# Linear attention and a mish FFN on one core: a staging room for the last group of part 1, and the first seven forms of part 2 spread over seven slots

## The chip, the cores and the metric

The kernel runs on one core of a Trainium2 chip. The metric is the device time of an execution in microseconds (us), the median of several runs. Engines are named as in the profile: PE (TensorE), DVE (VectorE), ACT (ScalarE), POOL (GpSimd), SP (SyncE). DMA transfers are issued here from SP and from ACT; each of the two has its own queue.

## What is computed

Two stages, on 8 batches, 8 heads, 576 positions and 64 columns a head, which make 4608 tokens of 512 columns:

```python
kv = np.einsum('bhsd,bhse->bhde', k, v)
out = np.einsum('bhsd,bhde->bhse', q, kv)
rms = np.sqrt(np.mean(out * out, axis=-1, keepdims=True) + 1e-06)
x = out / rms * g_norm                     # then (4608, 512)
h = x @ w_in                               # (4608, 2048)
g = h * np.tanh(np.log1p(np.exp(h)))       # mish
return g @ w_out                           # (4608, 512)
```

## The kernel before

Both products of the FFN are taken apart by a scheme with seven products of half-size blocks in place of eight. Each side of a product comes in seven "forms": `A11`, `S1`, `S2`, `A12`, `S4`, `S3`, `A22` (the order of `MADE`) for the activations, others for the weights. Four of them are blocks of the matrix, three are sums or differences of blocks. Each form is split into a high part (a cast on ACT, L117) and the rest (a subtraction on DVE, L118), and each product is three products of such parts on PE.

**Part 1** makes `g = mish(x @ w_in)` and writes it to DRAM (`gd`). It goes over nine tiles of 512 tokens, and in each over four column groups: 36 groups, "the last group" being the 36th. A group takes seven slots (`group`, p0 to p6), in each of which PE runs 12 products. In p2 a group also finishes the previous group's seventh product; the last group's seventh product follows at the very end by itself (`last_product`). Two tables, `plan` and `evict`, say which work of the other engines is written into which slot: `slot` first writes the evictions that are due, then the products, then the planned work. Every engine executes its instructions in the order in which they are written, so a slot is a place in each engine's order and not a time.

The result of a group is gathered in three staging tiles of the pool `up`: `ula` (block 11), `ulb` (block 21) and `ur` (blocks 12 and 22). Each name has two buffers, so a group reuses the buffers of the group two before it. ACT copies the first partial products into them (L460, L465, L474), DVE adds the others (L518), ACT takes the mish (L114, for `ulb` straight out of the PSUM bank), and three stores to `gd` follow (`put_in`: L521 for `ula`, L516 for `ulb`, L524 for `ur`, called the right store). In the last tile ACT issues these stores, elsewhere SP.

**Part 2** makes `g @ w_out` in 18 groups of 256 tokens. Its weights are in DRAM as forms already (`wod`) and come in eight loads (`wo_load`, L687), each into a buffer of `wfp` that part 1 has ceased to read. The first group of part 2 (`gs[0]`) goes over the contraction in four pairs of chunks (L815), pair 0 to pair 3, so that PE can begin before all weights are there. The forms of pair 0 are made in slot 18 of part 1's last tile, all seven at once (`g_pair`), in a room of their own (`g0`). Pairs 1 to 3 take two rooms each from `gf_room`: first the one for the forms `A11` to `A12`, then the one for the other three. `gf_room` deals out the four rooms of the pool `fp`, which part 1 has used for `x` and its forms, and one room of a pool `fp2`, in a cycle of five; the room of `fp2` comes first, sixth and so on. From the second group on (L733) each form takes one room, and ACT and DVE make forms three products ahead of PE (`AHEAD`). After each form `A22` SP loads the activations of a group further on (`g_load`, L692).

Each DMA counts on one of eight semaphores (DMAHW0 to DMAHW7 below). A transfer's issue also waits until an earlier transfer on the same semaphore has landed, where the engine doesn't know that already.

Of the kernel before, what the change touches and what calls it, by code (L numbers as in the profile page):

```python
# [7 lines left out]
F32 = mybir.dt.float32  # L8
F32R = mybir.dt.float32r
# [13 lines left out]
MADE = (A11, S1, S2, A12, S4, S3, A22)  # L23
# [3 lines left out]
def linear_attention_rms_mish_ffn(  # L27
# [38 lines left out]
    P = 128  # L66
    R = 32
    T = 512
    TH = T // 2
    NT = NTOK // T  # L70
# [3 lines left out]
    NQ = NF2 // 2  # L74
# [12 lines left out]
    fp = ctx.enter_context(tc.tile_pool(name="fp", bufs=4))  # L87
    fq = ctx.enter_context(tc.tile_pool(name="fq", bufs=1))
    up = ctx.enter_context(tc.tile_pool(name="up", bufs=2))
# [7 lines left out]
    pools = {}  # L97
# [18 lines left out]
    def split(hi, lo, src):  # L116
        nc.scalar.copy(hi, src)  # L117
        nc.vector.tensor_sub(lo, src, hi.bitcast(F32))  # L118
# [322 lines left out]
    def at(t, f):  # L441
        plan.setdefault(t, []).append(f)
# [59 lines left out]
    def u_dst(st, block):  # L502


        name, shape = {"11": ("la", TH), "21": ("lb", TH)}.get(block, ("r", T))
        if name not in st:
            st[name] = up.tile([P, 2, shape], F32, name="u" + name)
        return st[name] if name != "r" else st[name][:, :, (int(block[0]) - 1) * TH:int(block[0]) * TH]

    def put_in(st, block, bank, t):  # L510
        o, i, n = u_dst(st, block), st["i"], st["n"]
        eng = nc.sync if i < NT - 1 else nc.scalar
        left, right = gd[i][:, 2 * n:2 * n + 2, :], gd[i][:, NF2 + 2 * n:NF2 + 2 * n + 2, :]
        if block == "21":
            mish(o, bank)
            at(t + 2, lambda: eng.dma_start(left[:, :, TH:T], o))  # L516
            return
        nc.vector.tensor_add(o, bank, o)  # L518
        if block == "11":
            then(t + 1, lambda: mish(o, o))  # L520
            at(t + 3, lambda: eng.dma_start(left[:, :, 0:TH], o))  # L521
        elif block == "22":
            then(t + 1, lambda: mish(st["r"], st["r"]))
            at(t + 3, lambda: eng.dma_start(right, st["r"]))  # L524
# [147 lines left out]
    gs = [{"s": s, "f": {}, "bank": lambda name: ps_m.tile([P, 2, TH], F32, name=name)[:, 0]} for s in range(NG)]  # L672
    rooms_made = 0
# [6 lines left out]
    def gf_room():  # L680
        nonlocal rooms_made
        rooms_made += 1
        return (fp if rooms_made % 5 != 1 else pools["fp2"]).tile([P, 4, 2, 2, P], F32R, name="gf")

    def wo_load(c):
        wo[c] = wfp.tile([P, 7, 2, G], F32R, name="wf")
# [2 lines left out]
    def g_load(s):  # L689
        g = gs[s]["g"] = pools["gp"].tile([P, NFC, G], F32, name="g")  # L690
        i, h = divmod(s, T // G)
        nc.sync.dma_start(g, gd[i][:, :, h * G:(h + 1) * G])  # L692

    def g_block(st, f, cs):
        if f == S1:
            if st["s"] == 0:
                if cs.start not in st:
                    st[cs.start] = pools["g0"].tile([P, 2, P], F32, name="g1")
                return st[cs.start]
            if f not in st:  # L700
                st[f] = fq.tile([P, NF2, P], F32, name="a22")
            return st[f][:, cs]
        r, h = {A11: (0, 0), S2: (0, 0), A12: (1, 0), S4: (1, 0), S3: (0, 1), A22: (1, 1)}[f]
        return st["g"][:, r * NF2 + cs.start:r * NF2 + cs.stop, h * P:(h + 1) * P]

    def g_form(st, f, cs, t):

        a11, a12, a21, a22 = (g_block(st, f_, cs) for f_ in (A11, A12, S3, A22))
        if f == S1:
            nc.vector.tensor_add(g_block(st, S1, cs), a21, a22)  # L710
            nc.vector.tensor_sub(a21, a11, a21)
        elif f == S2:
            nc.vector.tensor_sub(a11, g_block(st, S1, cs), a11)  # L713
        elif f == S4:
            nc.vector.tensor_sub(a12, a12, a11)
        split(t[:, 0], t[:, 1], g_block(st, f, cs))
        return t

    def g_make(st, f):

        st["f"][f] = g_form(st, f, slice(0, NF2), gf_room().rearrange("p f s c n -> p (f s c n)").rearrange("p (s c n) -> p s c n", s=2, c=NF2))

    def g_pair(st, n, rooms):

        cs = slice(2 * n, 2 * n + 2)
        for f in MADE:
            st["f"][f, n] = g_form(st, f, cs, rooms[f // 4][:, f % 4])
# [38 lines left out]
    def pair_rooms(n):  # L766
        if n == 0:
            return [pools["g0"].tile([P, m, 2, 2, P], F32R, name=f"g{m}") for m in (4, 3)]
        return [gf_room() for _ in range(2)]


    t8 = NS * (NT - 1)
    at(t8 + 6, part2)
    at(t8 + 7, lambda: g_load(0))
    at(t8 + 8, lambda: g_load(1))
    at(t8 + 18, lambda: g_pair(gs[0], 0, pair_rooms(0)))
    for n in range(NQ - 1):
        for m in range(2):
            at(t8 + 7 * n + 10, lambda c=2 * n + m: wo_load(c))
# [2 lines left out]
    for i in range(NT):  # L782
        for n in range(NQ):
            st = {"i": i, "n": n, "bank": bank_new}
            t = NS * i + 7 * n
            for p, f in enumerate(group(st, t, mm_in, u_dst, put_in, prev)):
                slot(t + p, f)
            prev = st
# [14 lines left out]
    st = gs[0]  # L803
    for n in range(NF2 // 2):
        if n + 1 < NF2 // 2:
            g_pair(st, n + 1, pair_rooms(n + 1))
        for c in range(2):
# [3 lines left out]
            for (left, right), (b, h) in where.items():  # L811
                gf = st["f"][left, n]
# [92 lines left out]
```

## Time and profile before

| | us |
|---|---|
| median of 3 runs | 890.3 (888.53 to 890.5) |
| the profiled execution | 890.41 |
| its span, first to last instruction | 888.6 |
| part 2's first product (L815) | 517.86 |
| part 2's second group begins (L733) | 538.16 |

The mean granted clock of PE is 0.992. Times of the trace are counted from the first instruction, so 1.8 us of the profiled execution's time lie outside of them. In a row of the timeline stand start, duration, engine, line, operation, target and sources, and in brackets the idle time of the engine ahead of it with what ended it. "ACTq" and "SPq" are DMA issues. A row can hold several instructions of one kind (x12).

### The profile page before, as it was taken

Reading aid. Unit: us, or ns where it says so; the run is one execution under the profiler, and the core shown is the slowest. Engines: PE = TensorE matmul, PEld = TensorE weight load, DVE = VectorE, ACT = ScalarE, POOL = GpSimd, SP = SyncE. Lnnn points to the kernel's source line nnn. Section 1 sums busy time; section 2 is a strip of 40 time slices with the busy share of each in tenths; the row PEclk is TensorE's granted clock in tenths of the full one; section 3 lists DMA queues with packets and bytes.
Section 4 is the critical chain, followed back from the end, with each engine's and each line's share of the span. In section 5 each row is a group of like instructions: output and inputs, shape, how many; then the busy total and the mean of one; then the engine's idle time right before and its main releaser. Section 6 shows DMA issues by size and latency. Waiting matters only on the chain.

```text
span 888.6 us, 17122 instructions
## 1 busy us (share of the span) xinstructions
PE 827.8 (93%) x7004; PEld 793.5 (89%) x7004; DVE 614.2 (69%) x808; ACT 460.3 (52%) x698; POOL 4.3 (0%) x21
## 2 busy tenths in 40 slices
PE   1767899988999999999999899999999999999997
PEld 1456699988999999999899799999999999999997
DVE  4798685776777677777764358876766667776772
ACT  2565657566566765676665344434444443434431
POOL 1000000000000000000000000000000000000000
PEclk9999999999999999999999999999999999999999
DMA  9848598887979797767567994344444443334421
GB/s 285 252 134 259 154 291 253 254 254 232 284 231 301 226 270 213 215 205 213 192 202 241 420 421 151 119 128 154 152 137 124 134 124 119 119 119 135 153 69 48
DMA packets 154766, 177.42 MB, mean 200 GB/s; under 512 B 17408, under 2 KB 135168, under 8 KB 153664
## 3 DMA queue, kind: packets, MB, share of 16 engines
q1 hardware_dynamic: 151088, 170.59, 62.1%
q10 hardware_dynamic: 3600, 5.74, 1.9%
q8 instruction: 55, 0.90, 0.4%
q14 instruction: 23, 0.19, 0.1%
HBM read 114.30 MB, written 62.00 MB: 198 GB/s over the span
## 4 chain that ended last, share of the span: by engine, by line
PE 62%; DMA 13%; DVE 10%; ACT 8%; issue 4%; SPq 2%; ACTq 0%; DVEq 0%
PE a L733 21%; PE bc L733 16%; PE a L497 13%; PE bc L497 7%; DMA gd<-ula 4%; PE s L248 2%; DMA vm<-in_v_dram 2%; DVE ur L518 1%; DMA wf<-in_q_dram 1%; DMA gd<-ur 1%; DVE gf L118 1%; DMA wf<-in_k_dram 1%; ACT L382 1%; ACT gf L117 1%; DMA rd<-fl 1%
## 5 line engine op out<-in xcount | busy, mean ns | idle before, releaser
L733 PE MATMUL a<-wf,gf 128*128 128x256 f32 x1632 | 201.8, 283 | 0.5 <-DVE ur L764 0.5
L733 PEld LDWEIGHTS a<-wf,gf 128*128 128x128 f32 x1632 | 198.4, 192 | 0.7 <-DVE ur L764 0.7
L118 DVE TENSOR_TENSOR gf<-g,gf 128x1024 fp32r<-128x1024 f32 (+1 forms) x123 | 132.9, 1087 | 89.4 <-ACT gf L117 89.4
L497 PE MATMUL a<-gf,wf 128*128 128x256 f32 x1296 | 173.6, 288 | 9.8 <-ACT ur L474 4.4
L497 PEld LDWEIGHTS a<-gf,wf 128*128 128x128 f32 x1296 | 163.5, 193 | 16.9 <-ACT ur L474 6.9
L497 PE MATMUL bc<-gf,wf 128*128 128x256 f32 x1296 | 171.7, 285 | 7.0 <-DVE ula L518 2.6
L497 PEld LDWEIGHTS bc<-gf,wf 128*128 128x128 f32 x1296 | 162.4, 192 | 9.0 <-DVE ula L518 2.9
L117 ACT CAST gf<-g 128x1024 fp32r<-128x1024 f32 (+1 forms) x123 | 114.5, 939 | 93.4 <-DVE g L713 65.1
L733 PE MATMUL bc<-wf,gf 128*128 128x256 f32 x1224 | 152.7, 283 | 1.3 <-DVE gf L118 1.3
L733 PEld LDWEIGHTS bc<-wf,gf 128*128 128x128 f32 x1224 | 149.3, 192 | 1.7 <-ACT gf L117 1.0
L497 PE MATMUL a<-a,wf 128*128 128x256 f32 x432 | 58.5, 285 | 4.7 <-DVE ur L518 4.7
L497 PEld LDWEIGHTS a<-a,wf 128*128 128x128 f32 x432 | 54.7, 191 | 8.9 <-DVE ur L518 5.4
L114 ACT ACTIVATE ur<-ur 128x1024 f32<-128x1024 f32 x36 | 38.1, 1058 | 37.5 <-DVE ur L518 37.5
L118 DVE TENSOR_TENSOR fa<-fl,fh 128x1024 fp32r<-128x1024 f32 x28 | 34.2, 1223 | 20.7 <-ACT fh L117 19.7
L118 DVE TENSOR_TENSOR gf<-gf 128x512 fp32r<-128x512 f32 x45 | 30.4, 690 | 22.7 <-ACT gf L117 22.7
L117 ACT CAST gf<-a 128x1024 fp32r<-128x1024 f32 x17 | 17.9, 1052 | 53.4 <-DVE a L710 50.9
L465 ACT COPY ur<-bc 128x512 f32<-128x512 f32 (+1 forms) x53 | 27.4, 517 | 31.2 <-PE bc L733 23.0
L117 ACT CAST gf<-gf 128x512 fp32r<-128x512 f32 x45 | 27.1, 618 | 31.8 <-DVE gf L421 19.1
L474 ACT COPY ur<-a 128x512 f32<-128x512 f32 (+1 forms) x53 | 27.3, 515 | 30.3 <-PE a L733 24.6
L518 DVE TENSOR_TENSOR ula<-bc,ula 128x512 f32<-128x512 f32 x36 | 24.8, 688 | 24.7 <-PE bc L497 24.5
L114 ACT ACTIVATE ula<-ula 128x512 f32<-128x512 f32 x36 | 22.8, 633 | 22.1 <-DVE ula L518 22.1
L518 DVE TENSOR_TENSOR ur<-bc,ur 128x512 f32<-128x512 f32 x36 | 24.4, 678 | 11.1 <-PE bc L497 5.9
(128 smaller groups left out, 849.5 us busy)
## 6 DMA issues: line engine op xcount, KB each, us to landing
g<-gd SPq DMA_DIRECT2D x18, 2048.0 KB, 8.7
gd<-ur SPq DMA_DIRECT2D x32, 512.0 KB, 3.5
wod<-wst SPq DMA_DIRECT2D x16, 896.0 KB, 6.1
wf<-wod SPq DMA_DIRECT2D x8, 1792.0 KB, 15.4
gd<-ula SPq DMA_DIRECT2D x32, 256.0 KB, 5.5
gd<-ulb SPq DMA_DIRECT2D x32, 256.0 KB, 4.8
w<-in_moe_w_out_dram SPq DMA_DIRECT2D x32, 256.0 KB, 4.9
km<-in_k_dram SPq DMA_DIRECT2D x28, 256.0 KB, 4.3
```

The costliest lines, as they stand in the source:

```text
L114: nc.scalar.activation(o, i, AF.Mish)
L117: nc.scalar.copy(hi, src)
L118: nc.vector.tensor_sub(lo, src, hi.bitcast(F32))
L248: nc.tensor.matmul(kvps[o * D:(o + 1) * D, b % 2, h0 // 2 + i, :], kt, vt, start=(c == 0), stop=(c == CM))
L382: nc.scalar.preload_act_table_set("natural_log_exp_and_others")
L465: then(t + 2, lambda: nc.scalar.copy(dst(st, "22"), st["c"]))
L474: then(t + 4, lambda: nc.scalar.copy(dst(st, "12"), st["a"]))
L497: nc.tensor.matmul(bank[:, jj], w[:, right, a, kc, :], xf[:, b, kc, :], start=first and jj == kc == s == 0, stop=(kc == 1 and s == 2), ski ...
L518: nc.vector.tensor_add(o, bank, o)
L733: nc.tensor.matmul(bank, gf[:, a, c, :], wo[c][:, right, b, :], start=first and c == s == 0, stop=(c == NF2 - 1 and s == 2), skip_group_ch ...
```

## The change

Three edits. The last group's `la` and `r` no longer take buffers of `up`: one room of `fp2` of 1536 columns holds both. Its `lb` stays in `up`. `gf_room` takes the room of `fp2` as the fifth of the cycle and no longer as the first. And the seven forms of pair 0 are written one to a slot, in slots 17 to 23 of the last tile, in place of all in slot 18.

```diff
         if name not in st:
-            st[name] = up.tile([P, 2, shape], F32, name="u" + name)
+            if (st["i"], st["n"]) == (NT - 1, NQ - 1) and name != "lb":
+                if "room" not in st:
+                    st["room"] = pools["fp2"].tile([P, 2, 3 * TH], F32, name="gf")
+                st[name] = st["room"][:, :, 0:TH] if name == "la" else st["room"][:, :, TH:]
+            else:
+                st[name] = up.tile([P, 2, shape], F32, name="u" + name)
...
-        return (fp if rooms_made % 5 != 1 else pools["fp2"]).tile([P, 4, 2, 2, P], F32R, name="gf")
+        return (fp if rooms_made % 5 else pools["fp2"]).tile([P, 4, 2, 2, P], F32R, name="gf")
...
-    at(t8 + 18, lambda: g_pair(gs[0], 0, pair_rooms(0)))
+    first_rooms = []
+    for n, f in enumerate(MADE):
+        def first_form(f=f):
+            if f == MADE[0]:
+                first_rooms.extend(pair_rooms(0))
+            gs[0]["f"][f, 0] = g_form(gs[0], f, slice(0, 2), first_rooms[f // 4][:, f % 4])
+        at(t8 + 17 + n, first_form)
```

The order on PE and on SP stays as it was, row by row; only line numbers differ (from L518 on by 5, part 2's by 5 to 11). On DVE and ACT three places change.

DVE at the end of part 1, before: the second-to-last group's three additions (`ula`, `ur`, `ur`) behind the seven forms of pair 0. The tiles `g_` are the rooms of pair 0.

```order
L118 TENSOR_TENSOR g_5685<-g,g_5685 128x256 [waits DMAHW6_49,Activation_49]
L710 TENSOR_TENSOR g_5689<-g 128x256 [waits DMAHW7_49]
L711 TENSOR_TENSOR g<-g 128x2x128 [waits DVE_49]
L118 TENSOR_TENSOR g_5685<-g_5689,g_5685 128x256 [waits Activation_49]
L713 TENSOR_TENSOR g<-g_5689,g 128x2x128 [waits DVE_49]
L118 TENSOR_TENSOR g_5685<-g,g_5685 128x256 [waits Activation_49]
L118 TENSOR_TENSOR g_5686<-g,g_5686 128x256 [waits Activation_49]
L715 TENSOR_TENSOR g<-g 128x2x128 [waits DVE_49]
L118 TENSOR_TENSOR g_5685<-g,g_5685 128x256 [waits Activation_49]
L118 TENSOR_TENSOR g_5686<-g,g_5686 128x256 [waits Activation_49] x2
L518 TENSOR_TENSOR ula<-bc,ula 128x512 [waits DMAHW0_49,PE_49]
L518 TENSOR_TENSOR ur<-bc,ur 128x2x256 [waits DMAHW3_49,PE_49]
```

The same place on DVE now:

```order
L118 TENSOR_TENSOR g_5666<-g,g_5666 128x256 [waits DMAHW6_49,Activation_49]
L715 TENSOR_TENSOR g_5689<-g 128x256 [waits DMAHW7_49]
L716 TENSOR_TENSOR g<-g 128x2x128 [waits DVE_49]
L118 TENSOR_TENSOR g_5666<-g_5689,g_5666 128x256 [waits Activation_49]
L523 TENSOR_TENSOR ula<-bc,ula 128x512 [waits DMAHW0_49,PE_49]
L718 TENSOR_TENSOR g<-g_5689,g 128x2x128 [waits DVE_49]
L118 TENSOR_TENSOR g_5666<-g,g_5666 128x256 [waits Activation_49]
L523 TENSOR_TENSOR ur<-bc,ur 128x2x256 [waits DMAHW3_49,PE_49]
L118 TENSOR_TENSOR g_5667<-g,g_5667 128x256 [waits Activation_49]
L523 TENSOR_TENSOR ur<-a,ur 128x2x256 [waits PE_49]
```

The addition to `ula` stands behind the forms `A11` and `S1` alone, and the other two additions each behind one form more.

ACT in the last group of part 1, before: its copies out of the banks, and the issues of the second-to-last group's stores.

```order
L460 COPY ula<-a 128x512 [waits DMAHW5_49,PE_49]
L521 DMA gd_102<-ula 128x2x256 [waits DMAHW2_49,Activation_49]
L465 COPY ur<-bc 128x2x256 [waits DMAHW0_49,PE_49]
L114 ACTIVATE ulb<-a 128x512 [waits DMAHW4_49,PE_49]
L524 DMA gd_102<-ur 128x1024 [waits Activation_49]
L474 COPY ur<-a 128x2x256 [waits PE_49]
L516 DMA gd_102<-ulb 128x2x256 [waits DMAHW6_49,Activation_49]
```

The same now, from the copy into the new room (`gf`) on:

```order
L460 COPY gf<-a 128x2x256 [waits PE_49]
L117 CAST g_5667<-g 128x256
L526 DMA gd_102<-ula 128x2x256 [waits DMAHW2_49,Activation_49]
L465 COPY gf<-bc 128x2x256 [waits PE_49]
L117 CAST g_5667<-g 128x256
L114 ACTIVATE ulb<-a 128x512 [waits DMAHW4_49,PE_49]
L529 DMA gd_102<-ur 128x1024 [waits DMAHW5_49,Activation_49]
L474 COPY gf<-a 128x2x256 [waits PE_49]
L521 DMA gd_102<-ulb 128x2x256 [waits DMAHW6_49,Activation_49]
```

The two copies have lost their waits for a store, and the issue of the `ur` store has got the wait on DMAHW5 that the first copy had before; two casts of pair 0's forms now stand among them.

ACT at the beginning of part 2, before: the end of pair 2's casts, the last group's right store and its `ulb` store, and pair 3's first casts.

```order
L117 CAST gf<-g 128x256 x2
L524 DMA gd_102<-ur 128x1024 [waits DMAHW2_49,Activation_49]
L516 DMA gd_102<-ulb 128x2x256 [waits DMAHW3_49,Activation_49]
L117 CAST gf<-g 128x256
L117 CAST gf<-g_5997 128x256 [waits DVE_49]
```

The same now:

```order
L117 CAST gf<-g 128x256 x2
L529 DMA gd_102<-gf 128x2x512 [waits DMAHW2_49,Activation_49]
L521 DMA gd_102<-ulb 128x2x256 [waits DMAHW3_49,Activation_49]
L117 CAST gf<-g 128x256 [waits DMAHW2_49,DMAHW1_49]
L117 CAST gf<-g_5996 128x256 [waits DVE_49]
```

Pair 3's first cast has got two waits: DMAHW2 is the semaphore of the right store two rows above it, DMAHW1 that of the last group's `la` store.

## The prediction

> **What bounds the kernel now.** I read the page first, then TensorE's (PE's) timeline where part 1 passes into part 2, then ScalarE's (ACT's) there, then the chain of waits, then the landing times of the transfers. The page:
>
> ```profile
> span 888.6 us, 17122 instructions
> PE 827.8 (93%) x7004; PEld 793.5 (89%) x7004; DVE 614.2 (69%) x808; ACT 460.3 (52%) x698; POOL 4.3 (0%) x21
> gd<-ur SPq DMA_DIRECT2D x32, 512.0 KB, 3.5
> ```
>
> PE is busy for 93% of the span, so the change can only act where PE stands idle. PE's timeline around the passage (start, duration, what ended the idle time before):
>
> ```profile
> 497.38 3.04 PE L497 MATMUL a<-gf,wf 128*128 128x256 f32 x24
> 501.53 1.70 PE L497 MATMUL bc<-gf,wf 128*128 128x256 f32 x12 [1.12 <-DVE ula L518]
> 505.40 1.70 PE L497 MATMUL a<-gf,wf 128*128 128x256 f32 x12 [0.74 <-ACT ula L460]
> 510.91 2.33 PE L497 MATMUL bc<-gf,wf 128*128 128x256 f32 x12 [2.37 <-ACT ur L465]
> 513.04 2.50 PE L497 MATMUL a<-gf,wf 128*128 128x256 f32 x12
> 516.32 1.70 PE L497 MATMUL a<-a,wf 128*128 128x256 f32 x12 [0.78 <-DVE ur L518]
> 517.86 5.20 PE L815 MATMUL q<-wf,g 128*128 128x256 f32 x42
> 522.90 15.42 PE L815 MATMUL q<-wf,gf 128*128 128x256 f32 x126
> 538.16 3.04 PE L733 MATMUL a<-wf,gf 128*128 128x256 f32 x24
> 543.92 3.04 PE L733 MATMUL a<-wf,gf 128*128 128x256 f32 x24
> 547.44 3.10 PE L733 MATMUL bc<-wf,gf 128*128 128x256 f32 x24 [0.48 <-DVE gf L118]
> 551.37 3.10 PE L733 MATMUL bc<-wf,gf 128*128 128x256 f32 x24 [0.84 <-DVE gf L118]
> ```
>
> Four idle pieces stand in the last group of part 1 (1.12 + 0.74 + 2.37 + 0.78 = 5.01 us), none in the 20.3 us of L815, and two small ones in part 2's second group, where VectorE (DVE) makes the forms too late. What matters is which chain ends last at 551.37. The chain of waits there:
>
> ```profile
> 490.44 14.25 DMA gd<-ula
> 504.77 0.04 ACT ula L460
> 504.85 22.89 DMA gd<-ula
> 527.81 0.34 ACTq L524
> 528.24 0.42 ACTq L516
> 528.70 0.41 ACT gf L117
> 534.86 1.22 DVE gf L118
> ...
> 551.37 3.10 PE bc L733 x24
> ```
>
> The idle time in part 1 is not on it. It runs through two stores of the last tile: ACT can't issue the last group's right store (L524) until the store issued at 504.85 has landed at 527.74, and the forms of pair 3 (from 528.70) and of the second group stand behind that on ACT and DVE. So the passage is held by slow stores, and a gain in part 1 reaches the end only if this chain gets shorter as well.
>
> **The change part by part.**
>
> *One form per slot.* Before, seven forms stand in one block on DVE, and the evictions of the group before the last stand behind them; PE then waits 1.12 us at 501.53. With one form per slot (a slot is 12 products, half of the 3.04 us at 497.38), the addition to `ula` stands behind two forms, not seven, and is done before PE asks for that bank. No instruction is added. The 1.12 us go. Three slots of ACT take a little longer in their place, since the mish of that group and the copy that PE waits for at 505.40 now stand among casts of 0.4 us and behind the `ulb` store's issue; I leave the 0.74 us where they are (bounds 0 and 0.9).
>
> *Own staging.* It takes away the waits of ACT on the stores of two groups earlier (rows of ACT, then two stretches with each engine's busy time and, ahead of the last two columns, the granted clock):
>
> ```profile
> 499.41 0.37 ACTq L516 DMA_DIRECT2D gd<-ulb  x1
> 504.77 0.58 ACT L460 COPY ula<-a 128x512 f32<-128x512 f32 x1 [1.00 <-DMA gd<-ula]
> 510.28 0.58 ACT L465 COPY ur<-bc 128x512 f32<-128x512 f32 x1 [4.92 <-DMA gd<-ur]
> 521.78 0.58 ACT L114 ACTIVATE ulb<-a 128x512 f32<-128x512 f32 x1
> 528.70 0.41 ACT L117 CAST gf<-g 128x256 fp32r<-128x256 f32 x1 [1.28 <-DMA gd<-ula]
> 506.00:511.00 5.00, 2.63 (x23) 2.42 (x21) 0.69 (x1) 0.72 (x2) 0.00 (x0) 1.00 1.03 435
> 511.00:515.00 4.00, 4.00 (x22) 4.00 (x23) 0.69 (x1) 1.73 (x4) 0.00 (x0) 0.58 1.00 422
> ```
>
> The copy at 510.28 need no longer wait, so PE's 2.37 us go. With them goes a slow stretch: behind that idle time the granted clock is 0.58 (511 to 515), and 24 products take 513.04 + 2.50 - 510.91 = 4.63 us where the 24 at 497.38 take 3.04: 1.59 us. The 0.78 us at 516.32 stay, because the last product follows directly on the one whose bank DVE must read first. Part 2 then begins 1.12 + 2.37 + 1.59 = 5.1 us earlier, at about 512.8 in place of 517.86 (5.8 us earlier if the 0.74 go too).
>
> The Trainium skill ("TensorE: Matmul & The Clock Gate", "Part 1: The HAM clock gate") says that the clock falls to half after an idle window of some 3.4 us and comes back after such a window of work. Here the trace differs in the first half: 2.37 us of idle time in one piece were enough. By the rule alone there would be no slow stretch to win back, and part 2 would begin 3.5 us earlier in place of 5.1; the end, below, hangs on neither.
>
> *What of the 5.1 us survives.* Three things catch it, in this order. First, `ulb` is not restaged: the last mish (521.78 before) goes into the buffer that an earlier `ulb` store, issued at 499.4, still empties. ACT's stores land in their order here: the one ahead at 510.2 and the one behind at 527.74. I estimate its landing in the middle, at 519. Pair 2's forms, which stand behind this mish, so begin 521.78 - 519 = 2.8 us earlier, not 5.1. Second, the weights of part 2 still come over a full DMA:
>
> ```profile
> wf<-wod SPq DMA_DIRECT2D x1, 1792.0 KB, 15.3
> 518.06 0.32 SPq L687 DMA_DIRECT2D wf<-wod  x1
> gd<-ur ACTq DMA_DIRECT2D x1, 512.0 KB, 8.0
> gd<-ur ACTq DMA_DIRECT2D x1, 512.0 KB, 16.9
> 533.30 1.09 DVE L118 TENSOR_TENSOR gf<-g,gf 128x256 fp32r<-128x256 f32 x3 [0.47 <-ACT gf L117]
> 534.42 0.52 SPq L692 DMA_DIRECT2D g<-gd  x1
> 490.00:500.00 10.00, 10.00 (x85) 10.00 (x85) 3.35 (x9) 5.04 (x12) 0.00 (x0) 1.00 1.06 422
> 525.00:530.00 5.00, 5.00 (x44) 5.00 (x44) 3.11 (x9) 1.92 (x7) 0.00 (x0) 1.00 0.99 417
> 534.00:537.00 3.00, 3.00 (x26) 2.91 (x26) 2.53 (x4) 0.82 (x1) 0.00 (x0) 1.00 0.61 191
> ```
>
> The landing times are each the only one of its kind in a narrow window: the weight load of 518.06, the right store of 527.81, and the right store issued at 493.3. The last two columns of the window rows are the DMA engines' share and GB/s: full from 490 to 530 at 417 to 422 GB/s, free after about 534. The last weight load, issued at 518.06, lands 15.3 us later, at 533.4. Issued earlier, it still stands behind the same bytes, so its landing stays. PE needs it for the last eighth of L815's 168 products (20.3 us, so 2.5 us), and L815 can't end before 533.4 + 2.5 = 535.9: 2.3 us ahead of 538.16. That is a ceiling on any gain at this place.
>
> *The new wait.* The room is now the fifth in the cycle of rooms, the first of pair 3's two, and holds the last group's `la` and `r` until their stores have landed. So the first cast of pair 3 on ACT waits for the landing of the right store, the very store that could only be issued at 527.81. Before, that cast waited for the issue alone. Behind it on ACT stand the six other casts of pair 3, those of the second group and the copy out of L815's banks; DVE's subtractions wait for the casts one by one, PE for DVE, and SP's next load of the activations (534.42) for DVE's last read of the old ones. The profile has this store's time: issued at 527.81, landed 8.0 us later (third row), at 535.8. Its issue doesn't move, since it hangs on the store of 504.85: that one is issued at about 504.2 instead, but in ACT's queue it stays behind the two stores ahead, of which the nearer lands at about 519 either way, beside the same weight loads. So the cast starts at 527.8 + 8.0 + 0.1 = 535.9, where it started at 528.70: 7.2 us later. The bounds: 3.5 us to landing, the median of such a store on SP's queue (the page's row), gives 531.4 and 2.7 us; 16.9 us, the longest of the kind here (from 493.3 to 510.2, with weight loads all the way), gives 544.8 and 16.1 us. I take 8.0, because it is the same store against the same queue, which empties at about 534. In the changed layout its rows are 2 KB and no longer 4 KB; at a rate set by bytes that costs nothing, and I allow 0.5 us.
>
> *From there to the end.* Pair 3 takes the same instructions, 528.70 to 534.39 (the row at 533.30), now 535.9 to 541.6. PE has finished pair 2 at about 528 and stands idle for some 8 us, then goes at the pace of the forms; its last half of pair 3 (2.5 us) ends at about 544.4. The second group's forms follow on DVE as before, 7.2 us later; the load at 534.42 and its reader, the third group's first form, move alike. Their partner in the chain, the product at 551.37, comes at 558.6. PE at 544.4 has the 5.8 us of the first two products ahead of it and then meets the third form, before at 543.92 and now at 551.1 at the latest: it waits for DVE, not DVE for it. After 551.37 PE had 0.5 us of idle time in all, so nothing there gives the 7.2 us back.
>
> The sum against the profiled execution (890.41 us, of which 888.6 are the span): 890.41 + 7.2 = 897.6 us. The median of the three runs is 890.3, 0.1 us from it, so I let the number stand.
>
> **The rivals.**
>
> *The store lands in time (faster).* If the right store had landed by 528.7, the new wait would cost nothing, and the ceiling of the weights would decide: 890.4 - 2.3 = 888.1 us. For it speak the 5.1 us that part 1 surely saves. Against it: the store's issue at 527.81 and the shortest landing on the page, 3.5 us. It decides only if the store of 504.85 lands before about 520, some 8 us sooner than it did. Chance 0.05. Part of the way (the cast at 528 to 530) gives no change, 0.05.
>
> *The queue is empty sooner.* If the right store meets no weight load, it takes 3.5 us, and the cast comes 2.7 us later: 893.1 us. Against it: the last weight load lands at 533.4, so the store has company till then. The Trainium skill ("DMA: Bandwidth & Descriptors", "Queues, rings and completion order") says that a DMA engine takes turns between the rings that have work, a whole packet of some 9 to 17 descriptors at a turn; by that rule 256 KB in rows of 1 KB, 16 to an engine, would be through in about two turns. The trace speaks against so quick a passage: 22.89 us for the store at 504.85. Chance 0.09.
>
> *PE becomes the bound after its idle time (slower still).* After 8 us of idle time a slow stretch like that of 511 to 515 is to be expected. At half speed PE's last 2.5 us of pair 3 become 5, and another 3 us of work may take 6: L815 ends at 547 to 549 and the third product of the second group starts at 553 to 555 in place of 551.1. Part of that is hidden by the later forms, since DVE is late there; I put 1 to 3 us on top: 899 to 900.5. Chance 0.11. It decides when L815 ends later than about 546.
>
> **How the numbers follow.** My forecast, the new wait at its measured length, has a chance of 0.70: 897.6 us, with its own range 895.5 to 899. The range 892.8 to 900.5 takes in the quick queue and the slow clock, and leaves out the fast rival, no change and a store that takes much longer than 8 us. A measurement of this kernel tells about 0.2%, 1.8 us, from no change. Faster by more than that: 0.05; within it: 0.05; slower: 0.90.
>
> **What would show it.** Right: PE's idle times at 501.5 and 510.9 are gone and L815's first product starts at 512 to 513; ACT's first cast of pair 3 has a wait of about 7 us or more in front of it that ends with a store to `gd`, at about 536; PE has an idle piece of some 8 us in L815; all that follows is shifted by 7 us. Wrong: the cast of pair 3 starts before 531, or the idle piece in L815 is under 3 us, or part 1 still waits for stores.

## The result, and the profile after

| | before | changed |
|---|---|---|
| median of 6 runs | 890.06 us (888.31 to 890.5) | 895.72 us (894.8 to 898.07) |
| the profiled execution | 890.41 us | 894.8 us, the shortest of its six |
| its span | 888.6 us | 893.0 us |

The changed kernel is slower: the ratio is 1.0075, with a 95% interval of 1.0055 to 1.0094, which is 4.9 to 8.4 us; the two medians lie 5.7 us apart. Forecast were 897.6 us, or 7.2 us more.

PE's timeline of the changed kernel, the rows that answer to those of before (some rows without a wait are left out):

```profile
498.99 1.70 PE L497 MATMUL a<-a,wf 128*128 128x256 f32 x12 [0.23 <-DVE ur L523]
501.19 1.70 PE L497 MATMUL a<-gf,wf 128*128 128x256 f32 x12 [0.50 <-ACT gf L460]
502.73 3.04 PE L497 MATMUL bc<-gf,wf 128*128 128x256 f32 x24
507.99 1.69 PE L497 MATMUL a<-a,wf 128*128 128x256 f32 x12 [0.78 <-DVE gf L523]
509.52 5.20 PE L826 MATMUL q<-wf,g 128*128 128x256 f32 x42
521.69 4.22 PE L826 MATMUL q<-wf,gf 128*128 128x256 f32 x33 [0.71 <-DVE gf L118]
534.01 1.01 PE L826 MATMUL q<-wf,gf 128*128 128x256 f32 x3 [8.11 <-DVE gf L118]
536.82 7.03 PE L826 MATMUL q<-wf,gf 128*128 128x256 f32 x39 [1.79 <-DVE gf L118]
543.69 3.04 PE L738 MATMUL a<-wf,gf 128*128 128x256 f32 x24
555.78 3.10 PE L738 MATMUL bc<-wf,gf 128*128 128x256 f32 x24 [0.41 <-DVE gf L118]
```

The waits of 1.12 and 2.37 us are gone, and in their place stands an idle piece of 8.11 us in the fourth pair of the first group, with shorter ones of 0.71 and 1.79 us ahead of it and behind it. What holds it stands in ACT's timeline (some rows of it):

```profile
490.17 0.34 ACTq L529 DMA_DIRECT2D gd<-ur  x1
501.23 0.37 ACTq L526 DMA_DIRECT2D gd<-ula  x1
515.79 0.60 ACT L114 ACTIVATE ulb<-a 128x512 f32<-128x512 f32 x1 [1.99 <-DMA gd<-ulb]
525.04 0.37 ACTq L529 DMA_DIRECT2D gd<-gf  x1
533.10 0.40 ACT L117 CAST gf<-g 128x256 fp32r<-128x256 f32 x1 [11.65 <-DMA gd<-gf]
```

The cast at 533.10 is the first of pair 3. It waits for the store issued at 525.04, and that one could only be issued when the store of 501.23 had landed. The chain of waits names the same pieces:

```profile
501.23 23.74 DMA gd<-ula
525.00 0.04 issue
525.04 7.98 DMA gd<-gf
533.06 0.04 issue
533.10 0.41 ACT gf L117
...
555.78 3.10 PE bc L738 x24
```

**How to compare two traces here.** In eleven profiled executions the third-to-last group's `ur` store, the row at 490.17 above and at 493.26 before, is issued at 490.2 to 493.9 us, although the instructions up to it stand in the same order. The scatter is there among kernels without the staging as well (490.3 in e1, 493.9 in e8). So I count from that issue, called the mark. The row of before, and the same of three of the experiments told below:

```profile
493.26 0.34 ACTq L524 DMA_DIRECT2D gd<-ur  x1
```

```profile
490.27 0.34 ACTq L524 DMA_DIRECT2D gd<-ur  x1
```

```profile
492.59 0.34 ACTq L529 DMA_DIRECT2D gd<-ur  x1
```

```profile
491.94 0.34 ACTq L529 DMA_DIRECT2D gd<-ur  x1
```

They are before, e1, e2 and e10. All the times from the mark, in us: to part 2's first product, to pair 3's first cast, to the second group's first product, to its fifth (the one at 551.37 before and at 555.78 after), and to the end of the span:

| kernel | part 2 begins | pair 3's first cast | second group | its fifth product | end |
|---|---|---|---|---|---|
| before | 24.6 | 35.4 | 44.9 | 58.1 | 395.3 |
| changed | 19.3 | 42.9 | 53.5 | 65.6 | 402.8 |
| e1, spread forms alone | 24.4 | 35.7 | 45.1 | 58.3 | 395.6 |
| e2, staging alone | 19.5 | 43.3 | 54.7 | 66.3 | 403.4 |
| e3, room sixth | 19.4 | 35.8 | 51.2 | 63.4 | 400.7 |
| e4, room eighth | 19.0 | 35.8 | 47.2 | 58.7 | 395.9 |
| e5, eighth, two stores late | 19.3 | 31.0 | 43.0 | 57.6 | 394.9 |
| e7, ninth, all three late | 19.1 | 29.1 | 42.8 | 56.4 | 393.7 |
| e8, before with two stores late | 24.3 | 33.7 | 44.4 | 56.6 | 393.7 |
| e9, eleventh, all three late | 19.6 | 29.6 | 44.1 | 56.3 | 393.4 |
| e10, like e9, forms in a block | 19.5 | 29.5 | 43.0 | 54.5 | 391.6 |

Each row is one execution, and the twelve times of e9 alone lie 7 us apart (883.1 to 890.1), so a difference of 1 or 2 us between two rows carries weight only where the medians agree with it.

By this count the changed kernel's profiled execution is 402.8 - 395.3 = 7.5 us longer behind the mark, and begins 3.1 us earlier ahead of it. Pair 3's first cast comes 42.9 - 35.4 = 7.5 us later, and all that follows shifts by just that.

### The profile page after: what moved, and what is told of

It is laid out like the page before. It is cut to its first block, busy times and chain, and to the rows that moved or that the text cites. A ratio compares the mean times of both kernels' runs of the same rounds, so it can differ in the third digit from the quotient of the medians.

```text
span 893.0 us, 17122 instructions
## 1 busy us (share of the span) xinstructions
PE 828.5 (93%) x7004; PEld 795.4 (89%) x7004; DVE 614.5 (69%) x808; ACT 460.0 (52%) x698; POOL 4.3 (0%) x21
## 4 chain that ended last, share of the span: by engine, by line
PE 60%; DMA 14%; DVE 10%; ACT 9%; issue 4%; SPq 2%; ACTq 0%; DVEq 0%
PE a L738 21%; PE bc L738 16%; PE a L497 11%; PE bc L497 6%; DMA gd<-ula 3%; PE s L248 2%; DMA wf<-wod 2%; DMA w<-in_moe_w_in_dram 2%; DMA wod<-wst 1%; DVE ur L523 1%; DVE gf L118 1%; ACT L382 1%; DVE fa L118 1%; DMA w<-in_moe_w_out_dram 1%; DMA qs<-in_q_dram 1%
## 5 line engine op out<-in xcount | busy, mean ns | idle before, releaser
L117 ACT CAST gf<-gf 128x512 fp32r<-128x512 f32 x45 | 27.1, 619 | 33.0 <-DVE gf L421 19.1
L474 ACT COPY ur<-a 128x512 f32<-128x512 f32 (+1 forms) x52 | 26.7, 514 | 30.0 <-PE a L738 24.6
L523 DVE TENSOR_TENSOR ula<-bc,ula 128x512 f32<-128x512 f32 x35 | 24.1, 688 | 19.7 <-PE bc L497 19.4
L117 ACT CAST fh<-fl 128x1024 fp32r<-128x1024 f32 x28 | 29.4, 1049 | 0.0
## 6 DMA issues: line engine op xcount, KB each, us to landing
wod<-wst SPq DMA_DIRECT2D x16, 896.0 KB, 5.9
```

What stands on the lines that cost most here:

```text
L474: then(t + 4, lambda: nc.scalar.copy(dst(st, "12"), st["a"]))
```

## The experiments

**e1 and e2: the two halves of the change.** e1 has the third edit alone, e2 the first two. The diff of e2 against the changed kernel:

```diff
-    first_rooms = []
-    for n, f in enumerate(MADE):
...
-        at(t8 + 17 + n, first_form)
+    at(t8 + 18, lambda: g_pair(gs[0], 0, pair_rooms(0)))
```

Expected of e1:

> Only the seven forms of pair 0 one per slot; staging and rooms as in the kernel before. My theory (the loss is the new wait of pair 3's first cast for the right store): no loss and no gain. PE's wait of 1.12 us for DVE goes, but the copies still wait for stores, so part 2 begins within 1 us of before, and from the issue of the third-to-last group's ur store to pair 3's first cast it stays 35.4 us (528.70 - 493.26 before; 533.10 - 490.17 = 42.9 in the changed kernel). Median within 0.2% of before. Rival (the spread forms stand in the way of the evictions and make part of the loss): slower by 1 to 3 us.

Expected of e2:

> Staging and the new cycle of rooms, but all seven forms of pair 0 in one slot as before. My theory: nearly the whole loss, the same 42 to 43 us from the ur store's issue to pair 3's first cast, median 5 to 7.5 us over before. Rival (forms): most of the loss is gone, under 3 us.

Measured, against the kernel before run again beside each group of experiments: e1 889.23 us against 889.15 (ratio 0.9997, 0.9982 to 1.0012); e2 896.0 us (1.0072, 1.005 to 1.0094). PE in e1, in the last group of part 1:

```profile
502.24 1.70 PE L497 MATMUL a<-gf,wf 128*128 128x256 f32 x12 [1.67 <-ACT ula L460]
507.74 2.43 PE L497 MATMUL bc<-gf,wf 128*128 128x256 f32 x12 [2.36 <-ACT ur L465]
513.17 1.69 PE L497 MATMUL a<-a,wf 128*128 128x256 f32 x12 [0.78 <-DVE ur L518]
```

The wait of 1.12 us is gone, and the wait for `ula` behind it has grown from 0.74 to 1.67 us, since it ends with a store and not with DVE. So the spread forms alone change nothing, and the staging with its room makes the whole loss; pair 3's first cast comes at 43.3 in e2, as late as in the changed kernel. In e2 part 2 also begins as early as there (19.5 against 19.3 from the mark), although its wait of 1.12 us stays:

```profile
500.86 1.70 PE L497 MATMUL bc<-gf,wf 128*128 128x256 f32 x12 [1.12 <-DVE ula L523]
```

The wait of 0.74 us that before stood behind it is gone there. So the staging brings nearly all of part 1's gain by itself.

**e3 and e4: where the room stands in the cycle.** The changed kernel, and one line; for e4 with 8 and 3 in place of 6 and 1:

```diff
-        return (fp if rooms_made % 5 else pools["fp2"]).tile([P, 4, 2, 2, P], F32R, name="gf")
+        return (pools["fp2"] if rooms_made >= 6 and rooms_made % 5 == 1 else fp).tile([P, 4, 2, 2, P], F32R, name="gf")
```

> The changed kernel with the room of fp2 as the sixth of the cycle, so that the second room of pair 3 (forms S4, S3, A22) is the one that waits for the stores. My theory: pair 3's first cast starts right after the right store's issue again (35.4 to 36 us after the ur store's issue), and its fifth cast waits, 4.2 us further on in the changed kernel's own row of casts (537.26 - 533.10). So 4.2 us of the 7.5 us are won back: 3.3 us over before, 0.3 to 0.5% slower. Rival (PE's slow clock or the late weights make the loss): it stays at 5 us or more.

> The changed kernel with the room of fp2 as the eighth of the cycle: the second form of part 2's second group is the first to wait for the stores; its cast stands 8.6 us behind pair 3's first one (541.72 - 533.10), and the right store lands 8 us after its issue. My theory: the wait is covered, 0 to 0.5 us are left, median within 0.2% of before, no gain from part 1's 5 us, since pair 3's first cast still stands behind the right store's issue, which waits for an earlier store. Rival (the loss has another cause than the room): still 4 us or more slower. Second rival (the gain of part 1 reaches the end once the room is out of the way): 2 to 5 us faster.

Measured: e3 894.02 us (1.0044, 1.003 to 1.0058), e4 889.66 us (1.0, 0.9985 to 1.0016). ACT in e3:

```profile
527.49 0.37 ACTq L529 DMA_DIRECT2D gd<-gf  x1
528.45 0.41 ACT L117 CAST gf<-g 128x256 fp32r<-128x256 f32 x1 [3.93 <-issue]
529.69 0.41 ACT L117 CAST gf<-g 128x256 fp32r<-128x256 f32 x1 [0.83 <-DVE g L715]
530.92 0.40 ACT L117 CAST gf<-g 128x256 fp32r<-128x256 f32 x1 [0.83 <-DVE g L718]
536.19 0.40 ACT L117 CAST gf<-g 128x256 fp32r<-128x256 f32 x1 [4.87 <-DMA gd<-gf]
```

The wait has moved to the fourth cast, not the fifth that I expected: the rooms go by a form's number, in which S4 stands before A12, so a pair's first room holds A11, S1, S2 and S4 and its second A12, S3 and A22. (The description of `gf_room` above has this wrong too; the prediction doesn't use it.) The fourth cast is 2.8 us behind the first (in the changed kernel it is the second of two casts that take 0.71 us from 535.56 on, so it starts at about 535.9), not 4.2, and the store took 8.62 us to land here, not 7.98. So 7.5 - 2.8 + 0.6 = 5.3 us are left, and 400.7 - 395.3 = 5.3 were measured, where 3.3 were expected; the interval of the ratio, 2.7 to 5.2 us, reaches up to about that. The mechanism fits, with my number off by the mistaken form. But 5.3 us is also what the rival ("5 us or more") gave, so e3 speaks against it by the moved wait only, and e4 has to decide. In e4 the wait is gone:

```profile
527.96 0.37 ACTq L529 DMA_DIRECT2D gd<-gf  x1
528.42 0.48 ACTq L521 DMA_DIRECT2D gd<-ulb  x1
528.95 0.40 ACT L117 CAST gf<-g 128x256 fp32r<-128x256 f32 x1 [4.26 <-PE q L826]
```

The cast stands right behind the two issues again, whatever releaser the view names, and the time is that of before. Nothing but the place of one room in the cycle differs between 0.75% slower and no change. Part 1's gain of some 5 us (19.0 from the mark against 24.6) is still there in e4, and none of it arrives (395.9 against 395.3 at the end).

**e5 and e8: the issue of the right store.** Both have the last group's right and `ulb` stores written two slots later, which puts the right store behind five of pair 3's seven casts; e5 on e4, e8 on the kernel before.

```diff
-            at(t + 2, lambda: eng.dma_start(left[:, :, TH:T], o))
+            at(t + (4 if i == NT - 1 and n == NQ - 1 else 2), lambda: eng.dma_start(left[:, :, TH:T], o))
...
-            at(t + 3, lambda: eng.dma_start(right, st["r"]))
+            at(t + (5 if i == NT - 1 and n == NQ - 1 else 3), lambda: eng.dma_start(right, st["r"]))
```

> The room of fp2 as the eighth of the cycle, and the last group's right and ulb stores issued behind pair 3's casts on ACT. My theory (what eats part 1's gain once the room is out of the way is the wait of the right store's issue for an earlier store): pair 3's first cast comes about 31.5 us after the third-to-last group's ur issue (35.8 with the eighth room alone), but the right store now lands some 43 us after it and the second group's S1 cast, wanted at 40, waits for that; so 1 us faster than before, within 0.2%. Rival (the late weights hold the passage): the pair 3 cast comes earlier, but the end doesn't move at all, and PE's waits in L826 end with a weight load.

> The kernel before with only the right and ulb stores of the last group issued behind pair 3's casts; no staging, forms in one slot. My theory: pair 3's first cast comes 34.3 us after the third-to-last group's ur issue in place of 35.4, and the end 1 us earlier, within 0.2% of before. Rival (the issue's wait costs nothing): no difference at all; second rival (it is most of what holds the passage): over 2 us faster.

Measured: e5 888.35 us against 889.37 (0.9992, 0.9979 to 1.0006), e8 887.66 us (0.9984, 0.9971 to 0.9997). In e8 pair 3's first cast comes 33.7 us after the mark in place of 35.4, and the end moves by 395.3 - 393.7 = 1.6 us, somewhat more than the 1 us expected; the ratio's interval only just leaves out no change. What stood in front of that cast was only in small part the wait for a store. The last of pair 2's casts on ACT, before and then in the changed kernel:

```profile
526.40 1.02 ACT L117 CAST gf<-g 128x256 fp32r<-128x256 f32 x3 [0.98 <-DVE g L715]
```

```profile
520.43 1.02 ACT L117 CAST gf<-g 128x256 fp32r<-128x256 f32 x3 [0.98 <-DVE g L720]
```

Before, these casts end at 527.42 and the store landed at 527.74: 0.3 us of waiting, and then 0.9 us for the two issues, until the cast at 528.70. In the changed kernel they end at 521.45, and the issue comes at 525.04: there the wait is 3.6 us. In e5 the cast comes at 31.0, near the 31.5 expected, but the end gains only 0.4 us by the trace (1 us was expected), which the runs can't tell from no change. Two things are late at once:

```profile
527.05 0.37 ACTq L529 DMA_DIRECT2D gd<-gf  x1
535.58 1.05 ACT L117 CAST gf<-a 128x1024 fp32r<-128x1024 f32 x1 [6.39 <-DMA gd<-gf]
```

```profile
532.04 2.78 PE L826 MATMUL q<-wf,gf 128*128 128x256 f32 x21 [2.12 <-DMA wf<-wod]
```

The second group's S1 cast waits for the right store, which leaves no earlier than in e4 (35.3 us after the mark against 34.8), and PE waits for the last weight load.

**e7, e9, e10: all three stores late, and the room later still.** `lb` is staged in the room too, so that no mish waits for a buffer, and the `la` store is written four slots later, behind five of pair 3's casts, as well. The room is the ninth (e7) or the eleventh (e9, e10); e10 has the seven forms in a block again. Of the lines of e7 against the changed kernel that e5 hasn't shown, the two that say this:

```diff
-            if (st["i"], st["n"]) == (NT - 1, NQ - 1) and name != "lb":
+            if (st["i"], st["n"]) == (NT - 1, NQ - 1):
...
-            at(t + 3, lambda: eng.dma_start(left[:, :, 0:TH], o))
+            at(t + (7 if i == NT - 1 and n == NQ - 1 else 3), lambda: eng.dma_start(left[:, :, 0:TH], o))
```

> The room of fp2 as the ninth of the cycle, holding lb as well, and all three stores of the last group issued behind pair 3's casts. My theory: nothing on ACT waits for a store any more between pair 1 and pair 3; pair 3's first cast comes about 30 us after the third-to-last group's ur issue; then the last weight load, which lands about 40.5 us after that issue, holds PE, L826 ends 2.5 us later, and the kernel is 2.5 to 3.6 us faster than before (0.3 to 0.4%). Rival (DVE's forms or PE's slow clock hold it): under 1 us faster.

> As the all-late kernel with the ninth room, but the room of fp2 is the eleventh of the cycle, so that the second group's S4 form is the first to wait for the last group's stores. My theory (with the ninth room the second group's S2 cast waited 6 us for a store and gave half of the gain back; the weight loads then hold the passage): from the third-to-last group's ur issue to the end it takes 392.0 to 393.0 us (395.3 before, 393.7 with the ninth room), and the median is 0.35 to 0.45% under before. Rival (DVE's forms hold the second group by themselves): the same 393.7 as with the ninth room.

> The same kernel with the seven forms of pair 0 in one block again. My theory: part 2 begins about 1.1 us later (PE waits for DVE's addition to ula), but the last weight load still decides, so the end stays within 0.5 us of the kernel with spread forms. Rival (the spread forms carry part of the gain): 1 us or more slower than it.

Measured: e7 886.86 us against 889.37 (0.997, 0.9956 to 0.9985); e9 886.88 us against 888.74 (0.9975, 0.9957 to 0.9994); e10 885.34 us (0.9973, 0.9955 to 0.9992). All three beat the kernel before, and with it the changed one; the intervals don't tell them apart. PE's waits in e7, e9 and e10, in this order:

```profile
528.36 2.75 PE L826 MATMUL q<-wf,gf 128*128 128x256 f32 x21 [0.54 <-DMA wf<-wod]
533.55 2.77 PE L826 MATMUL q<-wf,gf 128*128 128x256 f32 x21 [2.44 <-DMA wf<-wod]
546.15 3.11 PE L738 MATMUL bc<-wf,gf 128*128 128x256 f32 x24 [0.83 <-DVE gf L118]
549.80 3.11 PE L738 MATMUL bc<-wf,gf 128*128 128x256 f32 x24 [0.55 <-DVE gf L118]
```

```profile
529.12 2.75 PE L826 MATMUL q<-wf,gf 128*128 128x256 f32 x21 [1.06 <-DMA wf<-wod]
533.86 3.66 PE L826 MATMUL q<-wf,gf 128*128 128x256 f32 x21 [2.00 <-DMA wf<-wod]
```

```profile
527.07 2.75 PE L820 MATMUL q<-wf,gf 128*128 128x256 f32 x21 [0.38 <-DVE gf L118]
532.29 2.78 PE L820 MATMUL q<-wf,gf 128*128 128x256 f32 x21 [2.47 <-DMA wf<-wod]
```

In each the last 21 products of the first group wait for a weight load, so the late weights do hold the passage once the stores are out of the way, and the second group begins 43 to 44 us after the mark. In e7 the S2 cast of that group still waited for a store (the two waits for DVE follow from it): by the medians e7 won the 2.5 us expected at the least, by its trace 1.6. In e9 no wait for a store is left, but its trace shows only 0.3 us of the 0.7 to 1.7 us expected over e7, and its median is 0.25% under before in place of 0.35 to 0.45%: after its idle pieces the last 21 products ran slowly, 3.66 us against 2.77. e10, without that, is at 391.6 us, 3.7 under before. So e9 doesn't show that the later room is worth anything over the ninth: 393.4 is about what the rival gave (393.7), though no wait for DVE stands in these rows of e9. e10's trace has a little more than was expected of e9 (392.0 to 393.0). A block of forms is no worse than the spread ones, once the staging is there: e10 is not slower. But the 1.1 us by which part 2 should begin later in e10 didn't come (19.5 us after the mark against 19.6), as e2 had shown already.

## Why the prediction was right, point by point

*One form per slot: 1.12 us go, about 0.74 us stay.* Right for the changed kernel as a whole: two short waits of 0.23 and 0.50 us in their place. But this edit isn't worth the 1.12 us that the sum gave it. Alone it brings nothing, since the next wait grows by as much (e1), and beside the staging it brings some 0.2 us: without it the 1.12 us stay and the 0.74 us go (e2). The prediction booked the two waits apart from each other and gave the staging no part in the second, though ACT's copy at 504.77, with which that one ended, had itself waited for a store.

*Part 2 begins 5.1 us earlier (5.8 at most).* Right: 24.6 - 19.3 = 5.3 us, by the mark; on the clock of the profile before that is 512.6, within the 512 to 513 given as a sign. By the previous point the number is in part luck: e2 has 5.1 us without the term of 1.12. The slow stretch behind the former wait is gone, as the 24 products at 502.73 show with their 3.04 us.

*What catches the gain: the `ulb` buffer, then the weights.* The first was right: the mish waited 1.99 us, until 515.79, which is 25.6 us after the mark, and my estimate of 519 was 25.7 after it. The ceiling of the weights could not be seen in the changed kernel, where the forms came later still; e5, e7, e9 and e10 show it: PE there waits for `wf<-wod`, and the second group begins 42.8 to 44.1 us after the mark where the ceiling of 535.9 is 42.6. The 2.3 us bound that place alone and not the end: e10's trace ends 3.7 us earlier, since DVE's waits in the second group are gone there too.

*The new wait: 8.0 us of landing behind an issue that doesn't move, 7.2 us in all.* Right in place, cause and size: 7.98 us of landing, the cast 7.5 us later by the mark. The difference of 0.3 us stands in the chain: the store of 501.23, issued 11.1 us after the mark and not 11.6, took 23.74 us and not 22.89, so the right store's issue came 34.9 us after the mark and not 34.6. That the issue doesn't move is borne out by e2, where the earlier store was issued 12.6 us after the mark:

```profile
505.19 22.15 DMA gd<-ula
```

It landed 34.7 us after the mark all the same, against 34.5 before and 34.8 in the changed kernel. The rows of 2 KB, for which I had allowed 0.5 us, cost 0 to 0.6: the right store takes 8.0 us in rows of 4 KB (before, e1) and 7.98, 8.41, 8.62 and 8.1 us in rows of 2 KB (changed, e2, e3, e4). e3 and e4 show that the room's place makes the loss: it shrinks when the room's first use is put off by one place, and at the eighth room it is gone within the runs' scatter.

*"The passage is held by slow stores."* Too strong for the kernel before: the wait for the store was 0.3 us there. But the conclusion drawn from it holds. Once part 1 is earlier the store does hold the passage, and e4 gains nothing from part 1's 5 us.

*From there to the end without change.* Right: 7.5 us at pair 3's first cast, 7.5 at the fifth product of the second group, 7.5 at the end. (Two slips of the working, on which nothing rests: 541.6 + 2.5 is 544.1 and not 544.4, and the DMA moved up to 435 GB/s between 490 and 530, as the row of 506 to 511 has it.)

*PE's slow clock as a rival.* It came, but didn't decide. The rows of the changed kernel with the granted clock ahead of the last two columns:

```profile
523.00:531.00 8.00, 2.91 (x25) 2.70 (x23) 0.00 (x0) 0.00 (x0) 0.00 (x0) 0.99 1.00 406
531.00:541.00 10.00, 5.15 (x20) 4.56 (x21) 5.98 (x13) 3.49 (x8) 0.00 (x0) 0.50 0.14 45
```

The granted clock stood at half from 531 to 541, of which PE was idle until 534.01 and for 1.79 us after that, and the second group began 53.5 - 44.9 = 8.6 us later than before. On the clock of the profile before that puts L815's end at 546.8, past the 546 from which the slow clock was to decide; it still cost nothing at the end. DVE's forms for that group were 7.5 us late themselves, and by the fifth product PE waited for DVE again (0.41 us at 555.78). The Trainium skill's rule of a cold clock after an idle window ("TensorE: Matmul & The Clock Gate", "Part 1: The HAM clock gate") agrees with this piece.

*The rival of a quick queue* (2.7 us) fell with the store's 7.98 us, and that of no wait at all with the idle piece.

The total, 895.72 us, is 1.9 us under the forecast, and 7.2 us lie inside the ratio's interval, 4.9 to 8.4 us. With a scatter of some 3.7 us ahead of the mark, six runs can't say more.

## What to carry to other kernels

When a buffer is lent to something that ends with a store, ask who takes that buffer next, and count from the store's issue: what the issue itself waits for, then its landing, beside what loads at that time. Removing a wait in front of a chain that runs through DMA brings nothing until the chain itself is shorter: here part 2 began 5.6 us earlier in e4, and the end didn't move. And an engine that both issues stores and makes forms should issue the stores that nobody waits for behind the forms that somebody does; that alone brought 0.16% in e8 (interval 0.03 to 0.29%).

## What the runs showed of the hardware that was not expected

A store of 256 KB from ACT took 22.9 and 23.7 us to land (501.23 above) while weight loads were queued on SP. On the page of before the median of 32 such stores, issued from SP in the other tiles, is 5.5 us:

```profile
gd<-ula SPq DMA_DIRECT2D x32, 256.0 KB, 5.5
```

The landings on ACT's queue that the changed kernel's trace shows keep the order of issue: 515.8, 525.0 and 533.0 for the stores issued at 496.54, 501.23 and 525.04. That each store there held up the next fits these times, and so does the right store of e7, e9 and e10: there the `la` store is issued 1.0 to 1.2 us ahead of it, where it was 9.2 us in the changed kernel, and the right store takes 10.1 to 10.2 us to land. It was not tried by itself.

The granted clock is not told by the length of the idle time alone: in e7 the last 21 products behind 0.54 and 2.44 us of idle time took 2.77 us, in e9 those behind 1.06 and 2.00 us took 3.66 us. Before, 2.37 us in one piece were followed by a clock of 0.58. The rows of e7 and of e9, with clocks of 1.00 and 0.67:

```profile
534.00:538.00 4.00, 4.00 (x36) 4.00 (x35) 1.98 (x2) 0.00 (x0) 0.00 (x0) 1.00 1.08 392
```

```profile
534.00:538.00 4.00, 4.00 (x25) 4.00 (x26) 1.99 (x2) 1.04 (x2) 0.00 (x0) 0.67 1.09 392
```

Why the clock fell in the one and not in the other was not tried.
